# Sliding-window attention into a star-ReLU layer: the order of the first loads of V and of the weights

## The chip, the cores and the metric

The kernel runs on one core of a Trainium2 chip. The metric is the device time of one execution in microseconds; the time before is the median of three runs. The profile is one further execution, recorded by the hardware profiler. A core has TensorE (PE; its weight loads are listed as PEld), VectorE (DVE), ScalarE (ACT), GpSimd (POOL) and SyncE (SP, which issues the DMAs), and 16 DMA engines.

## The reference

Eight batches of eight heads with 576 tokens of 64 elements: attention in a window of 32 tokens to either side, and then a two-layer block on all 4608 tokens, whose 512 features are the eight heads side by side.

```python
scores = np.matmul(q, k.transpose(0, 1, 3, 2)) / np.sqrt(64)
scores = np.where(np.abs(pos[:, None] - pos[None, :]) <= 32, scores, -1e9)
attn = np.exp(scores - scores.max(-1, keepdims=True))
attn = attn / (attn.sum(-1, keepdims=True) + 1e-9)
x = np.matmul(attn, v).transpose(0, 2, 1, 3).reshape(4608, 512)
h = np.maximum(x @ w_in, 0.0)             # w_in 512 x 2048
out = (s * (h * h) + b) @ w_out           # w_out 2048 x 512
```

q, k, v, the weights and the output are float32; s and b are single numbers.

## The kernel before

Everything is one program on one core. The matrix products run in bfloat16: each float32 input is loaded into a staging buffer and cast by POOL, ACT or DVE.

**Attention.** A batch has nine tiles of 64 queries, taken two at a time as five *units* (0 to 4). For the first two batches ("batch one" and "batch two" in the text, 0 and 1 in the code) the scores of a pair of heads are made for all units at once (`pair_scores`, L913); the last tile of batch one has its own scores (`late_scores`, L937 and L940, exponential at L950, mask on DVE at L953). For a unit, `av_part` multiplies the exponentials by V (L838), `finish` normalises (DVE, L860 and L862), transposes on PE (L869) and copies the result to XT (ACT, L877). q and k of a batch come as `q0`, `k0`, `q1`, `k1` (four heads each, L667) and `t` (the last 64 tokens of both, L655); they are cast (L645), transposed on PE (L672, L659) and copied out (L650, L651). V of a unit is one load of 256 KB (`load_v`, L588; for unit 4 half of it) and one cast (`cast_v`, L596 or L597).

**The layer.** Tokens go in blocks of 512. `s1` makes a hidden group: matmuls with w_in (L1092), ReLU on ACT (L1099), square on DVE (L1105). `second` multiplies by w_out for a block (L1149), in a form with seven products of half size instead of eight, for which DVE first makes sums of parts of w_out (`weight_sums`, L1121, which need all of w_out) and of the squares (L1141). `constant` multiplies w_out by ones (L1223) for the term with b; s and b come by two small loads into SROW (L1021) and are spread over the partitions by a stream shuffle on DVE (L1023). The results leave by L1165 and L1174. The first block is cut in three pieces of 224, 128 and 160 tokens, whose groups run in the order FIRST, by fourths of w_in.

**Weights.** w_in and w_out come in four parts of two loads each, 512 KB a load. The text calls the loads w0a, w0b to w3b and o0a to o3b. `load_weights` issues one (L560) and has POOL cast it (L563).

**What sets the order.** `add` puts each step on the list of an engine, with the tiles that it reads and writes, a cost and a key. `plan` then simulates the five engines and the DMA and fixes each engine's order: at each turn the step that can start first, the lower key among equals. At run time each engine follows its fixed list, and waits where its next step is not ready. Steps with a key under -100 form a chain: they are issued in the order in which they were added. All loads that take their key from `nxt()` are in that chain; they start at -199. The chain on SP before is: the eight pairs of q and k of batch one, then ORDER0, the two loads into SROW, ORDER1, all of w_out, and `t`, `q0`, `k0`, `q1`, `k1` of batch three (2 in the code). In ORDER0 a number under 8 is a unit's V, 8 and 9 are w0 and w1. V of batch three is not in the chain: it has a key from its due time and waits for attention units of the batches before (`paced`).

All loads but V share a ring of staging buffers (`stage`, 6144 columns; 1024 for a weight load, for `q0` and the like, 512 for `t` and for a pair), taken in the order in which the steps are added; a load waits for the cast that read its columns last. V has a buffer for each unit number.

Of the kernel before, what the change touches and what calls it, by code (L numbers as in the profile page):

```python
# [21 lines left out]
PAIRS = 3  # L22
# [2 lines left out]
LAG = 1  # L25
K0 = ("dve", "dve", "dve", "dve")
Q0 = ("act", "pool", "pool", "pool")
ORDER0 = (0, 8, 1, 2, "t", 3, 9, 4)
ORDER1 = ("t", "q0", "k0", "q1", "k1", "w2", "v0", "v1", "w3", "s", "v2", "v3", "v4")
WINE = ("pool", "pool", "pool", "pool")  # L30
SPLIT = {0: (224, 128, 160), 1: (256, 256), 2: (256, 256)}
FIRST = ((0, 0), (1, 0), (0, 1), (2, 0), (1, 1), (2, 1), (0, 2), (1, 2), (2, 2), (0, 3), (1, 3), (2, 3))
WOUTE = (("pool", "pool"),) * 4
SWITCH = 215.0
XTS = 4000.0
FOURS = ("t", "q0", "k0", "q1", "k1")
# [9 lines left out]
PACEV = ((-1,-1,0,0,1),(0,0,1,1,2),(0,0,1,1,2))  # L46
# [275 lines left out]
def bass_sliding_window_symmetric__then__act_starrelu_kernel(  # L322
# [23 lines left out]
    with ExitStack() as es:  # L346
# [227 lines left out]
        def late(b):  # L574

            return "sp" if b < LATE else "act"
# [417 lines left out]
        def attention():  # L994
            seq = {"k": -200.0}

            def nxt():
                seq["k"] += 1.0
                return seq["k"]

            def w(which, i):
                for x in (0, 1):
                    load_weights(which, i, x, nxt(), WINE[i] if which == "in" else WOUTE[i][x])

            for pr in range(NPAIR):
                for name in "qk":
                    load_pair(name, pr, nxt())
                    turn_pair(name, pr, -60.0 + 0.1 * pr, banks, K0[pr] if name == "k" else Q0[pr], 200.0)
                pair_scores(0, pr)
            for t in ORDER0:  # L1010
                if t == "t":
                    part(0, "t", nxt(), -23.5, banks, 200.0)
                    late_scores()
                elif t < 8:
                    load_v(0, t, nxt(), "sp")
                    cast_v(0, t, -28.0 + t, EV0[t], 300.0)
                else:
                    w("in", t - 8)
            first_units()
            for i, src in enumerate((moe_s, moe_b)):  # L1020
                add("sp", lambda e, i=i, src=src: e.dma_start(SROW[0:128:32, i:i + 1], src.partition_broadcast(4)),  # L1021
                    600.0, writes=[("SROW", i)], dma=("l", 1, 15.0), key=nxt())
            add("dve", lambda e: e.stream_shuffle(SB128[:, :], SROW[:, :], [0] * 32), 150,  # L1023
                reads=[("SROW", 0), ("SROW", 1)], writes=[("SB128", 0), ("SB128", 1)], key=P2[0, 0] - 8.0, slack=500.0)
# [36 lines left out]
            while last:  # L1061
                close()
            yield T
# [438 lines left out]
```

## Time and profile before

| | |
|---|---|
| median of three runs | 311.63 us (311.13 to 312.18) |
| the profiled execution | 311.91 us, of which the span is 310.2 us |
| granted TensorE clock, mean | 0.989 |
| DMA | 54.30 MB, mean 175 GB/s |
| one load of V on SP's queue | 256 KB, 4.6 us from issue to landing (median of 32) |
| one load of w_in or w_out | 512 KB, 7.4 us (median of 8 each) |

The span runs from the first to the last recorded instruction; what the time has beyond it lies around it. In a timeline, a line gives start and duration in microseconds, the engine, the source line, the operation, what it writes and reads, and in brackets how long the engine was idle ahead of it and what ended that. In a line for SP the duration is the time that the issuing took, including the time that SP stood at it. Shares of DMA above 1 come from transfers that overlap within an engine.

### The profile page before, as it was taken

The page shows a single profiled execution, that of the slowest core. Times are in us where ns is not written, and L with a number is a line of the kernel's source. Part 1 is how long each engine was busy: PE and PEld are TensorE (multiplying, and loading weights), DVE is VectorE, ACT ScalarE, POOL GpSimd, SP SyncE. Part 2 cuts the span into 40 slices and gives each one's busy share as a digit, 9 for nine tenths or more (in the row PEclk, how much of TensorE's full clock was granted, in tenths as well). Part 3 has the DMA queues.
Part 4 walks back from the last instruction along what each step waited for, and adds up shares of the span by engine and source line. Part 5 has one row for each costly group of instructions (what it writes and reads, how often), then busy time and mean ns, then how long its engine had stood idle before and what let it go on. Part 6 is the DMA issues. An engine that isn't in the chain of part 4 may idle for free.

```text
span 310.2 us, 8797 instructions
## 1 busy us (share of the span) xinstructions
PE 297.0 (96%) x3837; PEld 213.8 (69%) x3837; DVE 232.7 (75%) x401; ACT 157.2 (51%) x244; POOL 65.5 (21%) x79
## 2 busy tenths in 40 slices
PE   8877979999999999999999999999999999999994
PEld 3455867688888887676667666666666666666784
DVE  3546669899698789799978796977876785666673
ACT  3745856485986554655555345444544433333300
POOL 5424566500000243037016300270000000000000
PEclk9959999999999999999999999999999999999999
DMA  6999989999892997999699879999812110300223
GB/s 201 311 229 290 274 234 368 280 292 251 196 200 79 232 194 148 253 245 200 164 260 197 148 176 245 213 193 169 138 53 87 53 47 4 99 21 15 69 70 106
DMA packets 120153, 54.30 MB, mean 175 GB/s; under 512 B 94817, under 2 KB 115937, under 8 KB 120113
## 3 DMA queue, kind: packets, MB, share of 16 engines
q1 hardware_dynamic: 120112, 53.72, 72.3%
q8 instruction: 31, 0.51, 0.8%
q14 instruction: 10, 0.07, 0.1%
HBM read 36.70 MB, written 9.44 MB: 149 GB/s over the span
## 4 chain that ended last, share of the span: by engine, by line
PE 77%; DMA 10%; DVE 4%; POOL 2%; ACT 0%; issue 0%; POOLq 0%
PE o L1149 34%; PE w L1092 34%; DMA stg<-in_moe_w_in_dram 5%; PE avn L838 4%; DMA stg<-in_moe_w_out_dram 3%; DMA stg<-in_k_dram 3%; PE sc L780 2%; PE sc L1149 2%; PE avn L869 1%; DVE gt L1105 1%; DVE tw L1121 1%; POOL win L563 1%; POOL vb L597 0%; ACT r L1099 0%; DVE vb L597 0%; DVE wout L1121 0%
## 5 line engine op out<-in xcount | busy, mean ns | idle before, releaser
L1092 PE MATMUL w<-xt,win 128*128 128x512 bf16 (+4 forms) x832 | 144.8, 315 | 1.9 <-POOL win L563 1.7
L1099 ACT ACTIVATE r<-w 128x512 bf16<-128x512 f32 (+2 forms) x148 | 86.6, 586 | 103.1 <-PE w L1092 101.6
L1092 PEld LDWEIGHTS w<-xt,win 128*128 128x128 bf16 x832 | 75.2, 98 | 36.2 <-POOL win L563 1.7
L1105 DVE TENSOR_TENSOR gt<-r 128x1024 bf16<-128x1024 bf16 (+3 forms) x100 | 60.9, 617 | 28.4 <-ACT r L1099 27.7
L1149 PE MATMUL o<-wout,gt 128*128 128x256 bf16 x528 | 66.9, 273 | 0.4 <-DVE wout L1121 0.4
L1149 PEld LDWEIGHTS o<-wout,gt 128*128 128x128 bf16 x528 | 50.8, 98 | 13.8 <-DVE wout L1121 0.6
L732 POOL CAST nat<-stg 128x1024 bf16<-128x1024 f32 (+2 forms) x28 | 33.4, 1192 | 78.2 <-DMA stg<-in_q_dram 65.1
L808 ACT ACTIVATE ex<-sc 128x1024 bf16<-128x1024 f32 (+1 forms) x29 | 29.7, 1023 | 15.0 <-PE avn L838 9.8
L1149 PE MATMUL o<-tw,gt 128*128 128x256 bf16 x272 | 34.7, 273 | 0.0
L1149 PEld LDWEIGHTS o<-tw,gt 128*128 128x128 bf16 x272 | 26.2, 98 | 7.0
L1165 DVE SCALAR_TENSOR_TENSOR outs<-o,sb,cvec 128x512 f32<-128x512 f32 (+1 forms) x36 | 25.7, 714 | 4.8 <-PE o L1149 4.7
L1141 DVE TENSOR_TENSOR gt<-gt 128x1024 bf16<-128x1024 bf16 (+1 forms) x26 | 25.4, 978 | 0.3
L1165 DVE SCALAR_TENSOR_TENSOR outs<-o,sb,outs 128x512 f32<-128x512 f32 (+1 forms) x27 | 19.3, 715 | 6.8 <-PE o L1149 6.6
L838 PE MATMUL avn<-vb,ex 64*64 64x65 bf16 x944 | 20.1, 197 | 2.0 <-issue 1.4
L862 DVE TENSOR_TENSOR xn<-avn,rec 128x512 bf16<-128x512 f32 (+1 forms) x31 | 21.3, 686 | 0.7
L812 DVE TENSOR_TENSOR ex<-ex,mask 128x1024 bf16<-128x1024 bf16 (+1 forms) x29 | 21.3, 735 | 0.5
L838 PEld LDWEIGHTS avn<-vb,ex 64*64 64x64 bf16 x944 | 13.1, 106 | 11.7 <-issue 7.4
L597 DVE CAST vb<-vst 128x512 bf16<-128x512 f32 (+1 forms) x30 | 13.8, 464 | 6.3 <-DMA vst<-in_v_dram 6.3
L1149 PE MATMUL o<-tw,gsum 128*128 128x256 bf16 x136 | 17.5, 273 | 0.0
L1149 PEld LDWEIGHTS o<-tw,gsum 128*128 128x128 bf16 x136 | 12.8, 98 | 3.3
L1141 DVE TENSOR_TENSOR gsum<-gt 128x1024 bf16<-128x1024 bf16 x18 | 13.9, 774 | 0.3
L877 ACT COPY xt<-avn 128x512 bf16<-128x512 bf16 (+2 forms) x19 | 10.0, 533 | 4.9 <-PE avn L869 4.9
(119 smaller groups left out, 226.6 us busy)
## 6 DMA issues: line engine op xcount, KB each, us to landing
vst<-in_v_dram SPq DMA_DIRECT2D x32, 256.0 KB, 4.6
out_dram<-outs SPq DMA_DIRECT2D x32, 256.0 KB, 3.0
stg<-in_k_dram SPq DMA_DIRECT2D x24, 256.0 KB, 6.6
stg<-in_q_dram SPq DMA_DIRECT2D x5, 1024.0 KB, 7.0
stg<-in_moe_w_in_dram SPq DMA_DIRECT2D x8, 512.0 KB, 7.4
stg<-in_moe_w_out_dram SPq DMA_DIRECT2D x8, 512.0 KB, 7.4
stg<-in_q_dram SPq DMA_DIRECT2D x4, 512.0 KB, 7.6
stg<-in_k_dram SPq DMA_DIRECT2D x4, 512.0 KB, 8.1
```

Source lines behind the costliest of these rows:

```text
L597: (lambda e: e.tensor_copy(VB[0:n, vb, :, 0:D], VST[0:n, vs, :, :])),
L732: (lambda e, dst=dst, src=src: e.tensor_copy(dst, src)),
L808: add("act", lambda e, dst=flat_dst, src=flat_src: e.activation(dst, src, AF.Exp, bias=0.0, scale=0.125), 190 + 0.833 * 512 * len(hs), rea ...
L812: add("dve", lambda e, flat=flat, mask=mask: e.tensor_tensor(flat, flat, mask, ALU.mult), 130 + 0.53 * 512 * len(hs), reads=[("E", ei, hp, ...
L838: return [lambda e: e.matmul(av[64 * x:64 * x + 64, h, 0:D + 1], lhsT=buf[64 * g:64 * g + 64, h % 2, h // 2, c:c + 64], rhs=VB[64 * g:64 * ...
L862: add("dve", lambda e: e.tensor_tensor(XN[xi][0:p1, :].rearrange("p (a c) -> p a c", a=H), av[0:p1, :, 0:D], REC[ri][0:p1, :].rearrange("p ...
L1092: add("pe", [lambda e, g=g, kc=kc: e.matmul(wt[:, g, :], lhsT=WIN_BF[:, kc, (f0 + g) * 128:(f0 + g + 1) * 128], rhs=XT[:, kc, t0 % XR:t0 % ...
L1099: add("act", lambda e: e.activation(rt, wt, AF.Relu, bias=0.0, scale=1.0), 190 + 0.833 * ng * nt, reads=[("W", wb)], writes=[("R1", rb, ha ...
L1105: add("dve", lambda e: e.tensor_tensor(GT[gs][:, f1:f1 + nf, g0:g0 + nt], rr, rr, ALU.mult), 130 + 0.55 * nf * nt, reads=[("R1", rb, x) fo ...
L1141: add("dve", lambda e: e.tensor_tensor(dst, x, y, op), 1240.0 if half is None else 690.0, reads=reads, writes=writes, key=k)
L1149: add("pe", [lambda e, g=g, j=j, dst=dst: e.matmul(dst, lhsT=lhs[:, g, 128 * j:128 * j + 128], rhs=rhs[:, g, :], start=first and g == 0 an ...
L1165: add("dve", lambda e, src=src, dst=dst, other=other: e.scalar_tensor_tensor(dst, src, SB128[:, 0:1], other, ALU.mult, ALU.add), 200 + 1.0 ...
```

## The change

Three things are put in another order on SP's queue. In batch one and batch two the loads of V alternate with loads of weights, one by one: ORDER0 and ORDER1 name the two loads of a part (`a`, `b`) singly, and `w` becomes `weights`, which issues one of them. All of w_out is in ORDER1, its first three loads among V of batch two, and the two loads into SROW with the shuffle (`c`) stand behind the third of them. Batch three gets an order of its own, ORDER2: its V loads are now in the chain, unit 0 behind `k0` and the others behind `k1`, and no longer wait for `paced`. Engines, sizes and the number of the steps are the same, and so are the casts of V and their keys; the casts of weights keep their rule (the load's key plus 150). The order in which staging columns are taken follows the new order.

```diff
-ORDER0 = (0, 8, 1, 2, "t", 3, 9, 4)
-ORDER1 = ("t", "q0", "k0", "q1", "k1", "w2", "v0", "v1", "w3", "s", "v2", "v3", "v4")
+ORDER0 = ("v0", "w0a", "v1", "t", "w0b", "v2", "v3", "w1a", "v4", "w1b")
+ORDER1 = ("t", "q0", "k0", "q1", "k1", "w2a", "w2b", "v0", "w3a", "v1", "w3b", "s", "v2", "o0a", "v3", "o0b", "v4", "o1a", "c", "o1b", "o2a", "o2b", "o3a", "o3b")
+ORDER2 = ("t", "q0", "k0", "v0", "q1", "k1", "v1", "v2", "v3", "v4")
...
-            def w(which, i):
-                for x in (0, 1):
-                    load_weights(which, i, x, nxt(), WINE[i] if which == "in" else WOUTE[i][x])
+            def weights(step):
+                which, i, x = {"w": "in", "o": "out"}[step[0]], int(step[1]), "ab".index(step[2])
+                load_weights(which, i, x, nxt(), WINE[i] if which == "in" else WOUTE[i][x])
...
-            for i, src in enumerate((moe_s, moe_b)):
-                add("sp", lambda e, i=i, src=src: e.dma_start(SROW[0:128:32, i:i + 1], src.partition_broadcast(4)),
-                    600.0, writes=[("SROW", i)], dma=("l", 1, 15.0), key=nxt())
-            add("dve", lambda e: e.stream_shuffle(SB128[:, :], SROW[:, :], [0] * 32), 150,
-                reads=[("SROW", 0), ("SROW", 1)], writes=[("SB128", 0), ("SB128", 1)], key=P2[0, 0] - 8.0, slack=500.0)
             for step in ORDER1:
                 if step == "s":
                     yield S
-                elif step[0] == "w":
-                    w("in", int(step[1]))
+                elif step == "c":
+                    ... (the two loads into SROW and the shuffle, as above)
+                elif step[0] in "wo":
+                    weights(step)
...
-            for i in range(4):
-                w("out", i)
...
-                    for which in FOURS:
-                        part(b, which, nxt(), due(b, 0) - 4.0 + 0.1 * FOURS.index(which), banks2, 1500.0)
+                    for step in ORDER2:
+                        if step[0] == "v":
+                            load_v(b, int(step[1]), nxt(), "sp")
+                        else:
+                            part(b, step, nxt(), due(b, 0) - 4.0 + 0.1 * FOURS.index(step), banks2, 1500.0)
                 for i, u in enumerate(group_of(b)):
-                    load_v(c, u, due(c, u) - 35.0, late(b), [paced(b, PACEV[min(b, 4) - 2][i])])
+                    if b >= PAIRS:
+                        load_v(c, u, due(c, u) - 35.0, late(b), [paced(b, PACEV[min(b, 4) - 2][i])])
                     cast_v(c, u, due(c, u) - 4.0, EV2[i], SLACK[3])
```

More of the change, by code (lines that the diff above doesn't have):

```diff
@@ L1013, in attention @@
                     late_scores()
-                elif t < 8:
-                    load_v(0, t, nxt(), "sp")
-                    cast_v(0, t, -28.0 + t, EV0[t], 300.0)
+                elif t[0] == "v":
+                    u = int(t[1])
+                    load_v(0, u, nxt(), "sp")
+                    cast_v(0, u, -28.0 + u, EV0[u], 300.0)
                 else:
-                    w("in", t - 8)
+                    weights(t)
             first_units()
-            for i, src in enumerate((moe_s, moe_b)):
-                add("sp", lambda e, i=i, src=src: e.dma_start(SROW[0:128:32, i:i + 1], src.partition_broadcast(4)),
-                    600.0, writes=[("SROW", i)], dma=("l", 1, 15.0), key=nxt())
-            add("dve", lambda e: e.stream_shuffle(SB128[:, :], SROW[:, :], [0] * 32), 150,
-                reads=[("SROW", 0), ("SROW", 1)], writes=[("SB128", 0), ("SB128", 1)], key=P2[0, 0] - 8.0, slack=500.0)
             for step in ORDER1:
@@ L1027, in attention @@
                     yield S
-                elif step[0] == "w":
-                    w("in", int(step[1]))
+                elif step == "c":
+                    for i, src in enumerate((moe_s, moe_b)):
+                        add("sp", lambda e, i=i, src=src: e.dma_start(SROW[0:128:32, i:i + 1], src.partition_broadcast(4)),
+                            600.0, writes=[("SROW", i)], dma=("l", 1, 15.0), key=nxt())
+                    add("dve", lambda e: e.stream_shuffle(SB128[:, :], SROW[:, :], [0] * 32), 150,
+                        reads=[("SROW", 0), ("SROW", 1)], writes=[("SB128", 0), ("SB128", 1)], key=P2[0, 0] - 8.0, slack=500.0)
+                elif step[0] in "wo":
+                    weights(step)
                 elif step[0] == "v":
```

## The prediction

> **What bounds the kernel now.** I read the page first, for the share of each engine and the chain that ended last.
>
> ```profile
> span 310.2 us, 8797 instructions
> PE 297.0 (96%) x3837; PEld 213.8 (69%) x3837; DVE 232.7 (75%) x401; ACT 157.2 (51%) x244; POOL 65.5 (21%) x79
> PE 77%; DMA 10%; DVE 4%; POOL 2%; ACT 0%; issue 0%; POOLq 0%
> ```
>
> TensorE is busy for 297.0 of 310.2 us, so 13.2 us are all that any reordering of loads can win. The profiled execution took 311.91 us, 1.7 us beyond its span and 0.28 us above the median of 311.63 us. Next I asked for the busy time in stretches that cover the whole span (after each stretch its length, then PE, PEld, DVE, ACT, POOL, the granted TensorE clock, the DMA engines' busy share and GB/s).
>
> ```profile
> core 0: us, PE busy (x) PEld busy (x) DVE busy (x) ACT busy (x) POOL busy (x), PEclk, DMA share, GB/s
> 0.00:20.00 20.00, 16.45 (x224) 8.71 (x224) 8.99 (x28) 9.53 (x14) 8.58 (x24) 0.91 0.94 247
> 20.00:26.00 6.00, 4.57 (x44) 3.26 (x43) 1.17 (x6) 3.83 (x8) 2.46 (x3) 0.73 1.12 225
> 26.00:42.00 16.00, 14.78 (x290) 12.19 (x290) 12.62 (x23) 11.98 (x21) 8.01 (x9) 1.00 1.04 300
> 42.00:46.00 4.00, 2.38 (x104) 1.76 (x100) 1.86 (x5) 1.94 (x3) 3.12 (x5) 1.00 0.65 161
> 46.00:56.00 10.00, 9.47 (x161) 7.09 (x154) 9.31 (x17) 5.42 (x11) 6.42 (x8) 1.00 1.00 330
> 56.00:66.00 10.00, 9.57 (x82) 7.32 (x80) 9.10 (x12) 6.46 (x12) 2.89 (x3) 1.00 1.11 322
> 66.00:300.00 234.00, 233.56 (x2910) 168.16 (x2911) 185.81 (x307) 118.02 (x177) 34.01 (x30) 1.00 0.68 150
> 300.00:310.20 10.20, 6.19 (x57) 5.29 (x55) 3.87 (x8) 0.00 (x0) 0.00 (x0) 0.99 0.25 82
> ```
>
> PE's idle time is 3.55 us before 20, 1.43 to 26, 1.22 to 42, 1.62 to 46, 0.53 to 56, 0.43 to 66, 0.44 in the 234 us after that, and 4.01 in the tail. From 66 us on TensorE is the bound. Before that it depends on loads, and a shorter load phase pays only in so far as it closes idle time of PE. What the change can touch is the 5.23 us between 20 and 66. The timeline of PE says what each hole waited for:
>
> ```profile
> 25.62 1.83 PE L1092 MATMUL w<-xt,win 128*128 128x224 bf16 x24 [1.18 <-POOL win L563]
> ...
> 37.54 0.93 PE L1092 MATMUL w<-xt,win 128*128 128x224 bf16 x8 [0.52 <-POOL win L563]
> ...
> 44.64 0.22 PE L838 MATMUL avn<-vb,ex 64*64 64x65 bf16 x4 [1.37 <-issue]
> ...
> 55.24 0.61 PE L1223 MATMUL sc<-wout,onesw 128*128 128x512 bf16 x2 [0.39 <-POOL wout L563]
> ...
> 65.92 1.05 PE L1149 MATMUL o<-wout,gt 128*128 128x256 bf16 x8 [0.35 <-DVE wout L1121]
> ```
>
> Four of the five wait directly or at one remove for a weight. The fifth, 1.37 us, is put down to nothing visible; it lies in the stretch where DMA is at its emptiest, which single microseconds show:
>
> ```profile
> 42.00:43.00 1.00, 0.83 (x52) 0.60 (x48) 0.36 (x2) 0.72 (x1) 0.43 (x1) 1.00 0.53 107
> 43.00:44.00 1.00, 0.27 (x12) 0.16 (x12) 0.96 (x3) 0.78 (x2) 0.87 (x2) 1.00 0.67 145
> 44.00:45.00 1.00, 0.36 (x7) 0.32 (x8) 0.41 (x2) 0.00 (x0) 0.94 (x2) 1.00 0.44 49
> 46.00:47.00 1.00, 1.00 (x30) 0.96 (x23) 0.77 (x3) 0.46 (x1) 0.83 (x2) 1.00 1.03 397
> 55.00:56.00 1.00, 0.76 (x5) 0.51 (x6) 0.97 (x2) 0.00 (x0) 0.49 (x2) 1.00 0.42 76
> ```
>
> At 46 us, with w_out under way, the engines are busy (1.03) at 397 GB/s. At 42 to 45 and at 55 they are busy for half the time. SP's own timeline shows what it was issuing ahead of each dip:
>
> ```profile
> 28.71 3.49 SPq L588 DMA_DIRECT2D vst<-in_v_dram  x2
> 32.24 4.12 SPq L560 DMA_DIRECT2D stg<-in_moe_w_in_dram  x2
> 36.40 5.86 SPq L588 DMA_DIRECT2D vst<-in_v_dram  x3
> 42.31 4.16 SPq L560 DMA_DIRECT2D stg<-in_moe_w_out_dram  x6
> 46.51 5.54 SPq L588 DMA_DIRECT2D vst<-in_v_dram  x2
> 52.09 3.77 SPq L560 DMA_DIRECT2D stg<-in_moe_w_out_dram  x2
> ```
>
> Three V loads in a row hold SP for 5.86 us, two hold it for 5.54, while six weight loads need 4.16. So SP sits on a V that follows another V; when it gets through, what was queued has nearly drained, and the next transfer starts late. Each dip comes just after such a group. The working reading is that adjacent V loads open holes in the DMA stream, and the change separates them.
>
> **The change, part by part.** Prices of single loads come from POOL's casts that waited for them, so that their starts are landings:
>
> ```profile
> 24.52 1.04 POOL L563 CAST win<-stg 128x1024 bf16<-128x1024 f32 x1 [2.00 <-DMA stg<-in_moe_w_in_dram]
> ...
> 36.08 1.32 POOL L563 CAST win<-stg 128x1024 bf16<-128x1024 f32 x1 [0.33 <-DMA stg<-in_moe_w_in_dram]
> ...
> 39.97 1.15 POOL L563 CAST win<-stg 128x1024 bf16<-128x1024 f32 x1 [0.95 <-DMA stg<-in_moe_w_in_dram]
> 42.57 1.04 POOL L563 CAST win<-stg 128x1024 bf16<-128x1024 f32 x1 [1.45 <-DMA stg<-in_moe_w_in_dram]
> ...
> 47.33 1.04 POOL L563 CAST wout<-stg 128x1024 bf16<-128x1024 f32 x1 [0.43 <-DMA stg<-in_moe_w_out_dram]
> 48.65 1.12 POOL L563 CAST wout<-stg 128x1024 bf16<-128x1024 f32 x1 [0.28 <-DMA stg<-in_moe_w_out_dram]
> ...
> 60.07 1.11 POOL L563 CAST wout<-stg 128x1024 bf16<-128x1024 f32 x1 [0.40 <-DMA stg<-in_moe_w_out_dram]
> ```
>
> A half of a weight block (a weight load below) costs 48.65 - 47.33 = 1.32 us of stream when nothing disturbs it. Two V loads and one weight load take 39.97 - 36.08 = 3.89 us, so a V costs (3.89 - 1.32) / 2 = 1.29. The last weight load of w_in took 42.57 - 39.97 = 2.60 us with nothing ahead of it in the queue that belongs to V: 1.28 us of it is a hole, the aftermath of the pair issued at 28.71.
>
> *Batch two, w_in's last blocks and V.* The order w2a, w2b, v0, w3a, v1, w3b carries the same bytes up to w3b as before, and the pair is gone. I take the whole 1.28 us hole off w3b's landing. PE's idle time at 42 to 46 is 1.62 us, of which 1.37 has no visible releaser; if that is not data, nothing is won, if it is, all goes. I take 1.2, since the stretch coincides with the emptiest DMA and with the V casts that the following attention units need; bounds 0 and 1.62. V of units 3 and 4 arrives one and two weight loads later relative to the stream (1.3 and 2.6 us), which the earlier stream pays back; POOL, which casts both kinds, is busy for 6.42 of 10 us from 46 on and keeps up.
>
> *w2b.* The hole of 0.52 us at 37.54 shrinks by what the earlier stream gains: srow's two little loads leave it, and the V, V, t, V of batch one becomes V, w, V, t, w, V, V, w. I take 0.3, between 0 and 0.52.
>
> *w_out.* Two V loads of batch three leave the place ahead of the last two weight loads (2 x 1.29 = 2.58 us), with the dip at 55 behind them; with the holes closed, w_out should be complete 4 to 5 us before the 60.07 of the last row. PE has block two's first layer to do meanwhile, so all that this buys is the waits of 0.39 and 0.35: I take 0.5, between 0 and 0.74. What is late next after that is nothing but PE itself.
>
> *w1b behind v4.* This goes the other way: the hole of 1.18 us before 25.62 ends with the cast of 24.52, and now one V more, 1.29 us, stands ahead of that load. Against it, DVE's wait for srow goes from here, and with it what stood behind it, the masks of the late scores, on which the attention of units 3 and 4 depends:
>
> ```profile
> 25.70 0.01 DVE L1023 LOAD_MASK_SELECT sb<-srow  x1 [2.64 <-DMA srow<-in_moe_b_dram]
> ```
>
> So PE can have those two units to do in the hole, with V of unit 4 landing earlier. I take 0, between a loss of 1.29 and a gain of 0.6 (half the hole).
>
> *srow's new place.* The stream shuffle on DVE waits for srow where the planner thinks that it lands; it was 2.64 us too optimistic. At about 50 us a wait like that holds the squares (L1105), the reciprocals of attention and later the weight sums behind it. DVE has 0.69 us idle between 46 and 56 and 0.90 between 56 and 66: 1.59 that absorb such a wait, and the two V casts of batch three that ran ahead of the weight sums now run behind them. I charge 0.3, between 0 and 2.64 - 1.59 = 1.05.
>
> *Batch three's V.* Their waits on attention are gone, and they stand on SP behind its t, q and k. V1 to V4 form a group of four, so holes of the 42 us kind appear after 60 us, where 233.56 of 234 us of PE are busy on work already loaded. The order of staging buffers shifts as well: w2b now follows t and the first q of batch two, where the queue still holds the later q and k for some 5 us. Nothing for both, plus or minus 0.3.
>
> Sum: -1.2 - 0.3 - 0.5 + 0 + 0.3 = -1.7 us. The profiled execution would become 310.2 us, the median 309.9. The ends of the terms add to -3.8 and +2.6.
>
> **The rivals.** *No hole to close.* The V loads are slow by themselves, and their order cannot matter.
> The Trainium skill, DMA: Bandwidth & Descriptors, section "Why small descriptors are slow (HBM only)", puts the price of small pieces into each packet; by that alone the order would be worth nothing. The trace disagrees at 42 to 45 us, where the engines' share of 0.44 to 0.67 is not that of busy engines.
> Then only the 0.74 us of w_out's waits can go, and the 1.29 of w1b can stand against them: 311.63 give or take 0.9. For it speaks the word "issue" at 1.37 us; against it the three rows with an idle DMA.
>
> *DVE takes the wait over.* srow lands over 1.6 us later than planned, at a time when DVE is busy for 9.31 and 9.10 of 10 us. The weight sums, which released the first product at 65.92 with only 0.35 us of idle time in PE, then end late; PE stands still for up to 1.05 us, and the same planning error holds the V casts of units 3 and 4, which now come later, for a further load of 1.3. With none of the other gains that is +2.35 less the 0.74 that w_out's lead gives: 313.2. It decides once the delay exceeds w_out's lead plus the 1.59. For it speaks the 2.64 us wait; against it the lead of 4 us.
>
> *The front fails.* w1b is 1.29 us later and no unit fills the hole, and the clock drops:
>
> ```profile
> 20.38 1.68 PE L1092 MATMUL w<-xt,win 128*128 128x224 bf16 x8 [0.25 <-ACT xt L877]
> ...
> 22.99 1.02 PE L1092 MATMUL w<-xt,win 128*128 128x224 bf16 x8
> ```
>
> Eight such matmuls take 1.68 us at the low clock (0.73 on the mean of 20 to 26) and 1.02 at the full one, so the 24 after the hole would lose 3 x 0.66 = 2.0. Of 3.3 us, the holes that follow up to 56 (1.22 + 1.62 + 0.53) can absorb all, so this ends as 311.6 to 312.8, the gains used up.
> The Trainium skill, TensorE: Matmul & The Clock Gate, "Part 1: The HAM clock gate (the "warmup" mystery)", lets the clock drop only after an idle window of about 3.4 us, by which a hole of 1.18 + 1.29 would cost no clock and 2.0 us less; here the clock was low at 20.38 after idle time of PE that sums to 3.55 us over 20 us, in several pieces, so the trace leaves the danger open.
>
> *All holes go.* Every term at its good end: -3.8, or 307.8.
>
> **How the numbers follow.** The forecast, -1.0 to -3.0 around 309.9, gets 0.48; all holes gone 0.08; no hole to close and the mild half of the failing front, together within 0.3%, 0.19; DVE taking the wait over 0.14; the bad half of the front 0.11. About 0.3% (0.94 us) is what a measurement of this kernel tells from no change. Faster is 0.56, same 0.19, slower 0.25. The range from 308.2 to 313.2 leaves out about 6 in 100 below and 12 above.
>
> **What would show it.** Right: no two or three V loads of batch two adjacent on SP, no microsecond with a DMA share under 0.7 between 25 and 55; w3b cast near 41 instead of 42.57; the last w_out cast near 55 to 56 instead of 60.07; PE's idle time at 42 to 46 under 0.6, and that from 20 to 66 near 3.5 instead of 5.23; the time after 66 unchanged. Wrong: dips of the same depth elsewhere in the stream; the 1.37 us still there with w3b early; DVE waiting for srow over 1.6 us around 50; PE's first weight wait growing past 2 us; or new idle time of PE after 66, where I expect none.

## The result, and the profile after

The changed kernel takes 308.89 us (median of five runs, 307.63 to 309.07), the kernel before in the same session 311.14 us (five runs, 310.61 to 312.18). The ratio is 0.9913 with a 95% interval of 0.9885 to 0.9941: faster by 0.9%, 2.25 us between the medians and 2.7 us by the ratio. The forecast was 1.7 us and 309.9. The profiled execution took 308.89 us.

From the page of the changed kernel, the totals and the chain that ended last by engine:

```profile
span 307.2 us, 8786 instructions
PE 294.9 (96%) x3837; PEld 213.4 (69%) x3837; DVE 233.2 (76%) x401; ACT 156.7 (51%) x244; POOL 66.4 (22%) x79
PE 79%; SPq 4%; DMA 3%; DVE 2%; issue 1%; POOL 0%
```

DMA falls from 10% of the chain to 3%. The stretches of the changed kernel, cut as before (length, PE, PEld, DVE, ACT, POOL, granted clock, DMA share, GB/s):

```profile
core 0: us, PE busy (x) PEld busy (x) DVE busy (x) ACT busy (x) POOL busy (x), PEclk, DMA share, GB/s
0.00:20.00 20.00, 15.66 (x228) 8.13 (x232) 8.56 (x27) 11.54 (x18) 8.72 (x24) 0.98 0.97 250
20.00:26.00 6.00, 5.86 (x113) 4.72 (x114) 5.25 (x10) 1.56 (x3) 2.36 (x3) 0.77 0.97 230
26.00:42.00 16.00, 14.21 (x277) 11.71 (x275) 11.35 (x19) 13.21 (x23) 9.52 (x12) 1.00 1.11 329
42.00:46.00 4.00, 3.92 (x77) 3.58 (x78) 3.81 (x9) 2.16 (x6) 3.15 (x5) 1.00 1.14 270
46.00:56.00 10.00, 9.86 (x144) 7.54 (x142) 7.91 (x16) 5.45 (x11) 7.31 (x7) 1.00 1.09 331
56.00:66.00 10.00, 10.00 (x99) 8.37 (x97) 8.65 (x12) 8.45 (x14) 1.04 (x1) 1.00 1.08 273
66.00:297.00 231.00, 229.31 (x2866) 164.16 (x2864) 183.86 (x304) 114.34 (x172) 34.29 (x30) 1.00 0.70 150
297.00:307.20 10.20, 6.04 (x56) 5.18 (x53) 3.84 (x8) 0.00 (x0) 0.00 (x0) 0.95 0.25 81
```

PE's idle time from 20 to 66 us falls from 5.23 to 2.15 us (0.14, 1.79, 0.08, 0.14 and 0.00 in the five stretches). It grows elsewhere: from 3.55 to 4.34 before 20 us, and from 0.44 to 1.69 after 66. At 42 to 46 us the DMA share goes from 0.65 to 1.14. Single microseconds, same columns:

```profile
42.00:43.00 1.00, 1.00 (x16) 1.00 (x17) 1.00 (x2) 0.43 (x2) 0.87 (x3) 1.00 1.17 291
43.00:44.00 1.00, 1.00 (x15) 0.93 (x12) 1.00 (x4) 0.88 (x3) 1.00 (x1) 1.00 1.10 331
44.00:45.00 1.00, 0.93 (x37) 0.66 (x36) 0.81 (x3) 0.58 (x2) 0.87 (x2) 1.00 1.22 232
...
55.00:56.00 1.00, 1.00 (x11) 0.82 (x9) 0.43 (x1) 0.45 (x1) 0.50 (x1) 1.00 1.21 216
65.00:66.00 1.00, 1.00 (x12) 0.90 (x10) 1.00 (x2) 1.00 (x2) 0.00 (x0) 1.00 0.55 124
```

The dips of 0.44 to 0.67 are gone where weights are loading (the lowest of the single microseconds from 25 to 56 is 0.98, at 51); 0.55 now stands at 65 us, where all weights are cast and PE is full. SP's own timeline of the changed kernel says why:

```profile
35.46 0.47 SPq L589 DMA_DIRECT2D vst<-in_v_dram  x1
35.98 1.93 SPq L561 DMA_DIRECT2D stg<-in_moe_w_out_dram  x1
37.95 0.48 SPq L589 DMA_DIRECT2D vst<-in_v_dram  x1
38.47 1.70 SPq L561 DMA_DIRECT2D stg<-in_moe_w_out_dram  x1
40.21 0.61 SPq L589 DMA_DIRECT2D vst<-in_v_dram  x1
...
59.05 6.81 SPq L589 DMA_DIRECT2D vst<-in_v_dram  x4
```

Units 2 to 4 of batch two, 5.86 us of SP in a row before, take 0.47, 0.48 and 0.61 us between weight loads. SP's time has moved rather than gone: the weight loads behind them hold it for 1.93 and 1.70 us, and the five loads take 5.36 us (35.46 to 40.82). Two V loads of batch one, units 2 and 3, still stand next to each other; SP takes 1.44 us for both. The four of batch three in a row take 6.81 us and are followed by the dip. Weights land earlier from w2b on, by POOL's casts in the changed kernel:

```profile
25.37 1.04 POOL L564 CAST win<-stg 128x1024 bf16<-128x1024 f32 x1 [1.87 <-DMA stg<-in_moe_w_in_dram]
...
35.54 1.04 POOL L564 CAST win<-stg 128x1024 bf16<-128x1024 f32 x1 [0.39 <-DMA stg<-in_moe_w_in_dram]
...
40.30 1.04 POOL L564 CAST win<-stg 128x1024 bf16<-128x1024 f32 x1
...
56.28 1.04 POOL L564 CAST wout<-stg 128x1024 bf16<-128x1024 f32 x1 [0.77 <-DMA stg<-in_moe_w_out_dram]
```

w1b is 0.85 us later than before (24.52), w2b 0.54 earlier, w3b 2.27, the last of w_out 3.79. And what PE still waits for, on its timeline (the three longest waits from 18 us on):

```profile
19.43 0.94 PE L839 MATMUL sc<-vb,ex 64*64 64x65 bf16 x32 [1.43 <-POOL vb L598]
...
36.63 0.94 PE L1097 MATMUL w<-xt,win 128*128 128x224 bf16 x8 [1.05 <-POOL win L564]
...
208.09 0.32 PE L839 MATMUL avn<-vb,ex 64*64 64x65 bf16 x16 [1.62 <-issue]
```

The wait for w1b (1.18 us at 25.62) has shrunk to 0.21 us at 26.47, that for w2b has doubled in this profile, unit 2 of batch one waits for its V (the cast of 18.76 on POOL), and a wait appears 140 us behind the change. On DVE srow costs next to nothing:

```profile
48.45 0.01 DVE L1029 LOAD_MASK_SELECT sb<-srow  x1 [0.38 <-DMA srow<-in_moe_b_dram]
```

Adding up the columns that PE had streamed by a given time gives the lead over the kernel before at equal work:

```
at (us)     26    36    38    45    52    56    68 .. 205   from 212 on
lead (us)  2.1   2.7   1.3   2.9   3.1   3.7   4.4         3.1
```

So 2.1 us are there by 26 us, before any V of batch two. Up to 1.7 of that can be the clock, which in these two profiles ran at half for 6.8 us before (16.4 to 23.2) and 3.4 after (19.4 to 22.8). But a second profile of the changed kernel (below), at half clock for 6.8 us like the one before, is 1.6 us ahead at 26 us and 4.1 at 68, so that the clock makes up little of the lead. The wait for w2b takes back 1.4, which the rest of the load phase restores and raises to 4.4; the wait at 208 takes 1.2 back for good.

### The profile page after: what moved, and what is told of

It reads as the page before. It is cut to its first block, busy times and chain, and to the rows that moved or that the text cites. A ratio compares the mean times of both kernels' runs of the same rounds, so it can differ in the third digit from the quotient of the medians.

```text
span 307.2 us, 8786 instructions
## 1 busy us (share of the span) xinstructions
PE 294.9 (96%) x3837; PEld 213.4 (69%) x3837; DVE 233.2 (76%) x401; ACT 156.7 (51%) x244; POOL 66.4 (22%) x79
## 4 chain that ended last, share of the span: by engine, by line
PE 79%; SPq 4%; DMA 3%; DVE 2%; issue 1%; POOL 0%
PE w L1097 36%; PE o L1154 31%; PE avn L839 4%; SPq L714 3%; DMA stg<-in_moe_w_in_dram 2%; PE sc L1154 2%; PE sc L781 2%; PE avn L870 1%; PE sc L1228 1%; DMA vst<-in_v_dram 1%; DVE outs L1170 1%; DVE gt L1110 1%; SPq L887 0%; SPq L707 0%; POOL win L564 0%
## 5 line engine op out<-in xcount | busy, mean ns | idle before, releaser
L1110 DVE TENSOR_TENSOR gt<-r 128x1024 bf16<-128x1024 bf16 (+3 forms) x100 | 63.6, 639 | 24.9 <-ACT r L1104 24.2
L1146 DVE TENSOR_TENSOR gt<-gt 128x1024 bf16<-128x1024 bf16 (+1 forms) x26 | 23.8, 916 | 0.4
L813 DVE TENSOR_TENSOR ex<-ex,mask 128x1024 bf16<-128x1024 bf16 (+1 forms) x29 | 22.5, 775 | 0.6
L598 DVE CAST vb<-vst 128x512 bf16<-128x512 f32 (+1 forms) x30 | 13.1, 444 | 9.5 <-DMA vst<-in_v_dram 9.5
L1146 DVE TENSOR_TENSOR gsum<-gt 128x1024 bf16<-128x1024 bf16 x18 | 13.2, 731 | 0.3
```

Source lines behind the costliest of these rows:

```text
L813: add("dve", lambda e, flat=flat, mask=mask: e.tensor_tensor(flat, flat, mask, ALU.mult), 130 + 0.53 * 512 * len(hs), reads=[("E", ei, hp, ...
L1110: add("dve", lambda e: e.tensor_tensor(GT[gs][:, f1:f1 + nf, g0:g0 + nt], rr, rr, ALU.mult), 130 + 0.55 * nf * nt, reads=[("R1", rb, x) fo ...
L1146: add("dve", lambda e: e.tensor_tensor(dst, x, y, op), 1240.0 if half is None else 690.0, reads=reads, writes=writes, key=k)
```

## The experiments

Single runs of one kernel scatter by 1.5 us and more to either side (the kernel before: 308.92 to 313.74 in one session of 35 runs), so times below are medians and ratios to the kernel before of the same session, with 95% intervals. The theory was that both spacings count: V of batch two by the DMA holes, batch one's order by filling the hole of w1b.

**V of batch two adjacent again, all else as changed.**

```diff
-"w2a", "w2b", "v0", "w3a", "v1", "w3b", "s", "v2", "o0a", "v3", "o0b", "v4", "o1a", "c",
+"w2a", "w2b", "v0", "v1", "w3a", "w3b", "s", "v2", "v3", "v4", "o0a", "o0b", "o1a", "c",
```

> The changed kernel with one part undone: V of batch two adjacent again (two loads between w2 and w3, three between w3 and w_out), all else as changed, with nearly the same order on PE. Theory (adjacent V loads hold SP and open holes in the DMA stream, which PE pays at 42 to 46 us): dips of the DMA share under 0.7 come back at about 35 and 41 us, w3b's cast starts 1 to 1.5 us later than the 40.3 of the changed kernel, PE idles over 1 us between 38 and 46, and the time is 309.9 to 310.7, that is 1.0 to 1.8 us over the changed kernel. Rival (the same bytes take the same time in any order; the gain came from the front and from batch three's V): no dip that matters, time within 0.4 us of the changed kernel.

Measured: 309.87 us, 0.9951 (0.9912 to 0.9990). Its stretches:

```profile
36.00:38.00 2.00, 1.06 (x9) 0.69 (x8) 1.65 (x3) 0.82 (x2) 1.73 (x3) 1.00 0.76 233
38.00:40.00 2.00, 2.00 (x44) 1.35 (x43) 1.97 (x3) 1.85 (x4) 1.58 (x2) 1.00 0.71 227
...
42.00:44.00 2.00, 1.90 (x51) 1.76 (x40) 1.98 (x4) 1.32 (x3) 1.36 (x2) 1.00 0.85 196
```

and its SP queue:

```profile
30.32 2.22 SPq L589 DMA_DIRECT2D vst<-in_v_dram  x2
...
37.45 4.98 SPq L589 DMA_DIRECT2D vst<-in_v_dram  x3
```

The order alone brings the holes back, and w3b lands at 42.49 and is cast at 42.55, as before the change. SP goes through the first two of the three in 0.47 and 0.58 us and stands at the third, which has half the size, for 3.84 (in the kernel before 0.47, 0.64 and 4.67). That settles what makes the holes, and the other profiles agree: of the fourteen, the four of kernels with these V together (before, this one, and below batch one's order alone and V in halves) have microseconds between 25 and 56 with a share of 0.57 or less, and in the ten with V apart none is under 0.86. But PE does not stand still for 1.37 us in the hole: its idle time from 38 to 46 is 0.59 us. That stall, the largest term of the forecast, does not come with the holes.

**Batch one's order as before, all else as changed.**

```diff
-ORDER0 = ("v0", "w0a", "v1", "t", "w0b", "v2", "v3", "w1a", "v4", "w1b")
+ORDER0 = ("v0", "w0a", "w0b", "v1", "v2", "t", "v3", "w1a", "w1b", "v4")
```

> The changed kernel with batch one's order as before (v0, w0a, w0b, v1, v2, t, v3, w1a, w1b, v4). At 36 us of the kernel before, the changed one was 2.7 us ahead at equal work of PE, and gave back 1.4 of it at the wait for w2b. Theory (what the front wins is given back at the next wait for a weight): PE is up to 1.5 us later at 30 us, its wait for w2b near 36 us shrinks from 1.05 to under 0.3, time 308.7 to 309.4. Rival (the front decides, with the shorter stretch of low clock): the full 1.5 to 2 us are lost, 310.4 to 310.9.

Measured: 310.70 us, 0.9990 (0.9960 to 1.0020), as the rival had it. The weights land as in the changed kernel (w3b 39.72, last of w_out 56.30) and DMA stays full, yet next to nothing of the gain is left. On PE:

```profile
23.94 1.83 PE L1097 MATMUL w<-xt,win 128*128 128x224 bf16 x24 [0.48 <-POOL win L564]
...
45.72 0.71 PE L839 MATMUL o<-vb,ex 64*64 64x65 bf16 x32 [0.71 <-ACT r L1104]
...
62.26 1.05 PE L1154 MATMUL o<-wout,gt 128*128 128x256 bf16 x8 [0.54 <-DVE wout L1126]
```

With units 3 and 4 of batch one later (unit 3 starts at 25.70, after the change at 23.36, before it at 27.38), their work runs where PE was to run something else, and waits open behind it. That is not all of it. Measured by PE's weight loads, at points where both kernels have made the same ones, this kernel is 2.0 us ahead of the kernel before at 76 us (the changed kernel 4.4), and 0.9 of that goes at one wait for DVE, 80 us behind the loads:

```profile
144.89 0.40 PE L870 MATMUL avn<-ident,xn 128*128 128x128 bf16 x4 [0.82 <-DVE xn L863]
```

The planner lays PE's own list anew for every order. The changed kernel has the list of the kernel before from 76 us on, this one hasn't. How much of the lost gain is due to the loads, and how much to the list, isn't separated.

**srow ahead of batch two again, all else as changed.**

```diff
-ORDER1 = ("t", "q0", ... "o1a", "c", "o1b", ...
+ORDER1 = ("c", "t", "q0", ... "o1a", "o1b", ...
```

> The changed kernel with the two loads into SROW and their shuffle ahead of batch two's t again, as before. Theory (DVE's wait for srow delayed the masks of the late scores and the units 3 and 4, which then cannot fill PE's wait for w1b): DVE waits 1.5 to 3 us for srow near 24 us, PE's hole before the first group on w1 is back at about 1 us, but the wait for w2b hides most of it: 308.9 to 309.6. Rival (srow's wait was a bound of its own): 310.0 or more.

Measured: 310.23 us, 0.9928 (0.9883 to 0.9973), with runs from 305.71 to 311.73. The shuffle runs at 24.36 without a wait. Too wide to size this step; no cost of the new place shows.

**V of batch three by its due time again, all else as changed** (load_v of all later batches behind `paced`, none in ORDER2).

> The changed kernel with V of batch three out of the chain again: keyed by its due time and waiting for attention units, as before, while all the rest keeps the new order. Theory (w_out's end matters only through small waits, since PE has other work): two of those V loads stand among the w_out loads again, the last w_out cast starts 2 to 3 us after the 56.3 of the changed kernel, the time is 309.2 to 309.9. Rival (w_out's completion sets the end): the full 2.6 us of the two loads, 311.5. Second rival (the early V loads are harmless where they stood): 308.9.

Measured: 308.71 us, 0.9920 (0.9889 to 0.9950), as the changed kernel. Two V are back among w_out, whose last cast is at 57.70 instead of 56.28, and nothing comes of it. This part of the change buys nothing that shows.

**The changed kernel once more**, beside the next four.

> The changed kernel once more, on the chip and beside the runs of the kernels of this group, to have it and its spread where they are. Both theories: ratio to the kernel before 0.989 to 0.994. Of interest besides is whether PE's wait of 1.6 us near 208 us, ahead of attention of the last batch, is there again (1.0 to 2.0 us): if the lead won in front runs into the chain of the last batch's k and q, it has to be in most executions; if it was chance, it is gone.

Measured: 307.47 us, 0.9881 (0.9829 to 0.9933). Its wait at 208 is half as long:

```profile
207.58 0.32 PE L839 MATMUL avn<-vb,ex 64*64 64x65 bf16 x16 [0.82 <-DVE gsum L1146]
```

**Batch one's order alone** (the kernel before with the new ORDER0).

> The kernel before with batch one's new order alone (v0, w0a, v1, t, w0b, v2, v3, w1a, v4, w1b); srow, batch two, w_out and batch three's V stay as they were. Undoing this part took nearly all of the gain away (ratio 0.999). Theory now (batch one's order carries the gain by itself, as V1 and t come earlier and the masks of the late scores with them): 0.992 to 0.995, that is 1.6 to 2.5 us. Rival (both are needed: what the front wins is lost again at the holes that the adjacent V loads of batch two leave): 0.997 to 1.001.

Measured: 311.41 us, 1.0003 (0.9973 to 1.0033). The holes in DMA remain (share 0.81 at 40 to 42 us, 0.75 at 42 to 44), and on PE stands:

```profile
49.30 0.70 PE L839 MATMUL avn<-vb,ex 64*64 64x65 bf16 x24 [1.20 <-ACT xt L878]
...
65.31 1.05 PE L1152 MATMUL o<-wout,gt 128*128 128x256 bf16 x8 [0.41 <-DVE wout L1124]
```

The second is w_out's wait of before. The first is put down to ACT's copy, but that began at 46.49 and took 0.58 us; what PE waited for comes up under the last experiment. Here w3b is cast at 40.42 although the pair stands together; the hole follows behind it (share 0.42 at 41 us).

At equal work this kernel is 2.4 us ahead of the kernel before at 78 us and still so at 119. Then PE waits twice for other engines, in a part where its list has another order than before, and at 125 us 0.7 is left, at the end 1.2:

```profile
120.40 0.40 PE L870 MATMUL avn<-ident,xn 128*128 128x128 bf16 x4 [0.63 <-DVE xn L863]
121.70 1.67 PE L1095 MATMUL w<-xt,win 128*128 128x512 bf16 x7 [0.90 <-ACT xt L878]
```

So in this profile batch one's order does win time while the weights load; half of it is lost far behind them.

**V of batch two apart, alone** (the kernel before with the new ORDER1, srow still ahead of it).

> The kernel before with V of batch two between the loads of w2, w3 and w_out alone; batch one, srow and batch three's V as before. Theory of the prediction (the holes in the DMA stream at 42 to 45 us cost PE about 1.2 us by themselves): no dip of the DMA share under 0.9 over two microseconds between 28 and 50, PE idle under 0.6 at 38 to 46, ratio 0.994 to 0.997. Rival (without the front's lead PE has work for that time anyway and the earlier weights buy nothing): 0.998 to 1.001 although the dips are gone.

Measured: 310.54 us, 0.9964 (0.9939 to 0.9989). The DMA share is 1.03 or more in every two microseconds from 34 to 56. PE still waits 0.68 us for w1b, and for one V that now stands behind weights:

```profile
26.01 1.83 PE L1095 MATMUL w<-xt,win 128*128 128x224 bf16 x24 [0.68 <-POOL win L564]
...
48.04 0.71 PE L839 MATMUL o<-vb,ex 64*64 64x65 bf16 x32 [1.03 <-POOL vb L598]
```

**Both spacings, nothing else** (the kernel before with the new ORDER0 and ORDER1, srow and batch three as before).

> The kernel before with two parts of the change: batch one's new order, and V of batch two between the weight loads; srow ahead of batch two's t and batch three's V keyed and paced, as before. Alone the first gave 1.0003 and the second 0.9964. Theory (each needs the other: the front's lead is lost where adjacent V loads leave holes, and the closed holes pay only if PE has its front work done): together 0.988 to 0.993, all of the change. Rival (they only add up, and the rest comes from srow and from batch three's V): 0.995 to 0.999.

Measured: 309.74 us, 0.9936 (0.9903 to 0.9970), between the two expectations. Of 0.9%, the two spacings make 0.6; the interval holds the whole gain, too.

**Each V load in two halves of four heads** (the order of before).

```diff
-VST[p0:p0 + m, vs, :, :], v[b, :, 64 * j:64 * j + m, :].rearrange("h p d -> p h d"))
-for b, j, p0, m in at],
+VST[p0:p0 + m, vs, 4 * y:4 * y + 4, :], v[b, 4 * y:4 * y + 4, 64 * j:64 * j + m, :].rearrange("h p d -> p h d"))
+for b, j, p0, m in at for y in (0, 1)],
```

> The kernel before, in the old order throughout, with each load of V issued as two of four heads each: same bytes, same packets, same place. Theory (SP stands at a V load until there is room for the whole of it, so the queue has drained when it gets through; half the size gets through earlier): the dips at 36 to 38 and 42 to 45 us become shallower, the mean DMA share at 42 to 46 rises from 0.65 to over 0.85, w3's last cast starts 0.5 to 1.2 us before 42.57; SP spends 0.5 us more on each V. Ratio 0.994 to 1.000. Rival (the dips come from the V transfers themselves, 256 byte pieces in a row, however they are issued): dips as before at 0.65, ratio 0.999 to 1.004, or slower by the extra issues.

Measured: 317.69 us, 1.0200 (1.0165 to 1.0235), outside both expectations. Six half loads in a row hold SP for 6.38 us where three whole ones held it for 5.86, so what holds SP is not the number of loads. The DMA share at 42 to 46 us rises from 0.65 to 0.80 and w3b is cast at 42.04, 0.53 us earlier; up to about 150 us the kernel is level with before, although its profile has a second stretch at half clock (3.4 us from 44.8 on). The loss comes later, where PE waits for k's transposes, which stand behind more loads on SP:

```profile
179.41 0.32 PE L838 MATMUL avn<-vb,ex 64*64 64x65 bf16 x16 [1.29 <-DMA kt<-nat]
...
216.75 0.32 PE L838 MATMUL avn<-vb,ex 64*64 64x65 bf16 x16 [2.80 <-DMA kt<-nat]
```

**w1b ahead of v4, all else as changed.**

```diff
-ORDER0 = (... "w1a", "v4", "w1b")
+ORDER0 = (... "w1a", "w1b", "v4")
```

> The changed kernel with one swap in batch one: w1b ahead of v4 instead of behind it; V1 and t stay early. The prediction charged 0 for this place, between a loss of 1.29 and a gain of 0.6 us. Theory (PE's hole before the first group on w1 is filled by units 3 and 4, so their V is worth as much as w1b): ratio to before 0.988 to 0.995, within 0.9 us of the changed kernel, PE's wait for w1b under 0.6 us. Rival (v4 ahead of w1b is what makes batch one's order worth its gain): 0.996 to 1.000, with PE waiting over 1 us for V of unit 4 or for w1b between 22 and 28 us.

Measured: 309.27 us, 0.9932 (0.9906 to 0.9958), within the noise of the changed kernel. PE doesn't wait for w1 here, and in the changed kernel for 0.21 us.

**w0b ahead of v1 and t, all else as changed.**

```diff
-ORDER0 = ("v0", "w0a", "v1", "t", "w0b", "v2", ...
+ORDER0 = ("v0", "w0a", "w0b", "v1", "t", "v2", ...
```

> The changed kernel with w0b back ahead of v1 and t in batch one; v1, t, v2, v3, w1a, v4, w1b follow as they come. Undoing all of batch one's order gave 0.999 in the changed kernel, swapping w1b and v4 alone 0.993. Theory (what batch one's order is worth lies in V of unit 1 and t landing one weight load, 1.3 us, earlier, with the first scores and masks behind them): most of it goes, ratio to before 0.996 to 1.000. Rival (the place of t ahead of v2 is enough, or the 0.999 had other reasons): 0.989 to 0.995.

Measured: 309.46 us, 0.9917 (0.9887 to 0.9947): the rival held, this move isn't what counts. Between this kernel and the one with all of batch one's old order there remain `t` ahead of v2 and w1b behind v4, and the latter alone changed nothing. So it is `t`, the two together, or PE's list, which differs too; that wasn't tried.

**The changed kernel with the last batches paced one step earlier**, to see what the wait at 208 is worth.

```diff
-PACE = ((-1, -1, -1),) * 3
+PACE = ((-1, -1, -1), (-1, -1, -1), (-2, -2, -2))
```

> The changed kernel with the loads of q and k of batches four and later (4 to 7 in the code) bound to an attention unit one earlier than before (PACE -2 for -1), so that the planner may put them earlier on SP. Theory (the lead of 4.4 us at 68 us falls to 3.2 at PE's wait near 208 us, where attention of the last batch waits for transposes whose chain on SP has not moved up as far): that wait shrinks from 0.8 to 1.6 us to under 0.4, the kernel wins 0.5 to 1.2 us over the changed one, ratio 0.985 to 0.990. Rival (the planner's other orders shift, SP's stores come later and the wait appears elsewhere): 0.990 to 0.996.

Measured: 310.19 us, 0.9942 (0.9908 to 0.9975). No wait over 0.3 us is left at 208, and the kernel is not faster: in the new order PE waits 1.56 us for DVE at 144.29. The profile shows something else besides, in a part where PE's order is that of the changed kernel:

```profile
47.86 0.24 PE L1097 MATMUL w<-xt,win 128*128 128x160 bf16 x1
49.42 1.21 PE L1097 MATMUL w<-xt,win 128*128 128x160 bf16 x15 [1.32 <-issue]
```

PE stops after one of sixteen like matmuls, with nothing to release it, while the DMA share from 48 to 50 is 1.05. The stall of the kernel before, too, lies within the 32 matmuls of one unit, as its weight loads show (PEld):

```profile
42.98 0.18 PEld L838 LDWEIGHTS avn<-vb,ex 64*64 64x64 bf16 x12 [0.21 <-PE avn L838]
44.64 0.11 PEld L838 LDWEIGHTS avn<-vb,ex 64*64 64x64 bf16 x4 [1.48 <-issue]
```

Counting PE's instructions (matmuls, weight loads and the few semaphore instructions between them) from the start gives 1217 up to that stop and 1473 up to the one here, 256 apart. The page of every kernel lists a queue on which instructions come:

```profile
q8 instruction: 31, 0.51, 0.8%
```

31 packets of 16 KB for PE's 7674 matmuls and weight loads, one for each 248. The trace has their times. Beside PE's stops they read as follows (PE runs dry where the last weight load ends; PE itself is idle for up to 0.2 us less; counts to within one instruction):

```
                         instructions   PE runs dry   packet lands      PE goes on
before                   1217           43.16         42.24 to 43.43    44.64
before                   1473           50.45         48.26 to 49.21    50.62
V in halves              1217           42.07         40.39 to 41.45    42.82
V in halves              1473           50.78         48.67 to 49.62    50.92
batch one's order alone  1473           47.93         47.10 to 48.13    49.30
the change, again        1473           47.62         45.56 to 46.73    48.08
w1b ahead of v4          1473           48.18         46.10 to 47.22    48.47
paced earlier             449           19.25         16.85 to 18.15    19.50
paced earlier            1473           47.95         46.84 to 48.06    49.41
the change               1473           no stop       44.42 to 45.98    (at 47.7)
```

Six profiles stop at three places that lie 256 instructions, or a multiple of it, apart, and each time PE goes on 1.17 to 1.41 us after the packet's end. All fourteen profiles together have 406 such places, and at none does PE go on earlier than about 1.1 us after its packet. While the weights load, the packets come late: between 35 and 56 us a packet starts 3.3 us (median) after PE has passed the place 256 instructions ahead of the one that it is for, at 70 to 120 us 0.8 after that, and from 200 us on mostly before PE is there. In the kernel before, the packet of the long stop starts 4.7 us after PE has passed that place; in the other thirteen profiles the same packet starts between 1.4 us ahead of it and 4.0 us after. So PE waited for its own instructions. This was read from fourteen profiles and not brought about by an experiment of its own.

## Why the prediction was right, and where it wasn't

**The reading of SP and DMA: shown.** Adjacent V loads open holes and weights between them close them. Putting V together again reopened the holes, and separating it in the kernel before closed them. Every sign named for it came: w3b at 40.30 (forecast near 41), the last of w_out at 56.28 (55 to 56), idle time at 42 to 46 of 0.08 (under 0.6), no microsecond from 25 to 56 with a share under 0.7. That the hole always costs w3b its 1.28 us is not so: with batch one's order alone w3b is cast at 40.42 beside adjacent V.
The Trainium skill, DMA: Bandwidth & Descriptors, section "Why small descriptors are slow (HBM only)", charges small pieces to each packet; here the same packets in another order raise the share from 0.65 to 1.14, so that what a packet costs isn't all, and the measurement decides.

**Batch two's V, -1.2: the step that failed in its reasoning.** The forecast took 1.2 of the 1.62 us because the 1.37 us without a releaser "coincides with the emptiest DMA". It is gone, but the kernel with the holes put back doesn't have it, and one without holes has the like at 49.42. By the table above it was a wait for a packet of instructions: how long it lasts hangs on when that packet gets through, and the longest of them is 0 and 0.31 us in the two profiles of the changed kernel and 1.37 in the one before. What the spacing is worth has to be read from the times instead: 0.9964 alone, and 0.9951 against 0.9913 and 0.9881 where it is taken out again; some 1 to 2 us, with intervals that overlap. The leads at 75 us agree: 0.9 us alone, 1.5 to 1.7 where it is taken out (table below). How much of that is fewer such stops stays open.
The Trainium skill, Runtime: NRT & Kernel Launch, section "Instruction fetch mechanics", has instructions streamed in blocks of 16 KiB, 256 of them, at a cost that is mostly hidden. The trace agrees on the block; hidden it was in eight profiles of fourteen, and in the others it cost 0.2 to 1.4 us.

**w1b behind v4, 0: mis-sized as a hole, right as an order.** The swap by itself moves nothing, as forecast. But the idle time from 20 to 26 fell by 1.29 us, as units 3 and 4 now fill the hole; "half the hole" was the far end of the bound, and it went whole. Part of it came back ahead of 20 us (+0.79), where unit 2 waits 1.43 us for its V, which now stands behind `t`. The rival's price of the low clock, 2.0 us for 24 matmuls, was read from a row that is not wholly at full clock (22.99, with half clock up to 23.2); eight at full clock take 0.94 us (at 28.55), which makes it 2.2.

**w2b, -0.3: wrong sign in the first profile.** The wait grew from 0.52 to 1.05 us. The cast came 0.54 us earlier, but PE came earlier still: a gain ahead of a load that hardly moves is turned into a wait for it. The time was made good after 38 us. In the second profile of the changed kernel w2b is cast at 34.69 and PE doesn't wait for it at all, so the sign isn't settled.

**w_out, -0.5: right, too small.** PE's idle time from 46 to 66 fell from 0.96 to 0.14, by 0.8.

**srow, +0.3: too dear.** DVE waited 0.38 us instead of 2.64, and no wait of PE follows from it; the rival built on it did not come.

**Batch three's V, 0: confirmed** by the kernel without that part (0.9920 against 0.9913).

**After 66 unchanged: wrong.** A lead of 4.4 us at 68 became 3.1 at 212. The unit there needs k's transposes, and SP, with its own chain of transposes, V and results, had gained less: the transpose of k that starts at 207.11 started at 210.19 before, 3.1 us. The wait is 1.62 us in one profile and 0.82 in the other of the same kernel, and the kernel without it was no faster, as it waited for DVE at 144 and for instructions at 49 instead; whether a second gain lies there stays open.

**The sum.** Terms of idle time from 20 to 66 add to 3.1 us instead of 1.7; 0.8 ahead of 20, 1.3 after 66 and 0.1 in the tail stand against them: 0.9 us. The spans of the two profiles differ by 3.0, so that 2.1 us lie in PE's busy time (297.0 against 294.9), which the forecast held constant. In these two profiles the half clock near 20 us lasts 6.8 us before and 3.4 after, which is 1.7 of it; but the second profile of the changed kernel has 6.8 us again and took 308.13 us, less than the first. So the gain does not hang on the clock, and the 2.1 us of busy time can't be booked to a term.

**What the forecast lacked** is what one part does to the other, and to PE's list. By the times, batch one's order is worth nothing alone (1.0003) and 0.8% within the change (0.9990 against 0.9913). V apart is worth 0.4% alone, and both 0.6%. That pair alone does not show that parts fail to add: 1.0003 times 0.9964 is 0.9967, inside the interval of both (0.9903 to 0.9970). The profiles, one each, show the lead over the kernel before at equal work:

```
                                   idle to 66 us   lead at 75   at the end   ratio
before                                  8.8
batch one's order alone                 8.3           2.4          1.2       1.0003
V of batch two apart, alone             9.0           0.9          1.3       0.9964
change without batch one's order        8.6           2.0          1.4       0.9990
change without V of batch two apart     8.9           2.6          2.1       0.9951
change without batch three's V          8.0           3.9          3.0       0.9920
both spacings only                      6.3           4.7          4.5       0.9936
the change                              6.5           4.4          3.1       0.9913
the change, second profile              6.7           4.1          3.7       0.9881
```

Where the loads end, batch one's order is worth 2.4 us alone and 2.1 to 2.3 within the change; V apart 0.9 and 1.5 to 1.7. So in the profiles each part pays by itself. With batch one's order alone, 1.7 us of the lead then go between 119 and 125 us, at the two waits for DVE and ACT, and without it 0.9 at the wait at 145; both kernels have another list on PE there. V apart alone, V together again and the change keep the list of the kernel before from 76 us on. That the front pays only together with V apart is therefore not shown; orders of loads with PE's list held fixed were not run. PE's idle time is no measure of it: the change without batch three's V idles for 8.0 us and has the whole gain. In these profiles, before and the first of the change apart, five or six records of matmuls ahead of 66 us are missing, which at the length of their neighbours counts 0.35 to 0.65 us of work as idle. And one profile is one execution: that of both spacings took 307.65 us against a median of 309.74, so that single leads are good to a microsecond or two. The rival of a failing front had it right that gains ahead can be used up by waits that follow, but these came after 66 us, where it had none.

## What to carry to other kernels

Where one queue issues both loads of many small pieces and loads of few large ones, put a large one between any two of the small kind, and look at the issuing engine's own timeline: time it spends standing at a load shows as a hole in the DMA some microseconds later. Here the order by itself was worth 0.4%. Before a stall without a releaser is booked to such a hole, count PE's instructions up to it: where such stops lie 256, or a multiple of it, apart, PE waits for instructions that come late beside the data. And test a reordering with its parts alone as well as taken out, and compare the lists of the other engines: where a planner lays them anew for each order, a gain can be lost far behind the loads that won it.

## What the runs showed of the hardware that was not expected

- SP took 0.47 to 0.61 us for a V load between weight loads in the changed kernel, and 4.98 to 6.81 us for three or four in a row. In a row of three it stood at the last, of half the size, for 3.84 to 4.82 us. Halves didn't shorten it (6.38 us for six), so it goes neither by the number of loads nor by the size of the one that it stands at.
- PE ran out of instructions for up to 1.4 us in 6 of 14 profiles, only at its 449th, 1217th or 1473rd, while loads filled the DMA, and went on 1.17 to 1.41 us after a 16 KB packet of instructions had landed.
- The half clock near 20 us lasted 3.4 or 6.8 us in profiles of the same kernel, and the time did not follow it (308.89 and 308.13 us).
